# v in 512-byte runs with its key halves swapped on chip, and expert matrices loaded in halves through attention

## The chip, the cores and the metric

The kernel runs on one core of a Trainium2 chip. The metric is the device time of one execution in microseconds (us). All tensors are 32-bit floats. The compute engines are TensorE (PE in the profile; its weight loads are PEld), VectorE (DVE), ScalarE (ACT) and GpSimd (POOL). SyncE (SP) issues every transfer. Each engine works through its own list in order and waits, where it must, on semaphores of the others and of the transfers.

## The reference

Three stages follow each other: attention inside chunks of 64 positions, a soft mixture of eight experts over all 4608 tokens, and a two-layer softplus block.

```python
# q, k, v: (8 batches, 8 heads, 576 positions, 64)
scores = scale * q_c @ k_c.T            # per chunk of 64 positions, 9 chunks
attn = softmax(scores); out = attn @ v_c
x = out as (4608, 512)
logits = x @ phi                        # 512 x 32 slots, 4 per expert
d = softmax of logits over the tokens; slot_input = d.T @ x
h = relu(slot_input[e] @ w1[e]); slot_out[e] = h @ w2[e]     # 8 experts, 512x1024 and 1024x512
y = softmax of logits over the slots @ slot_out
return softplus(y @ w_in) @ w_out       # 512x2048 and 2048x512
```

The slot inputs are sums over all tokens, so no expert product can begin before the last attention output is known. The expert matrices themselves, 16 blocks of w1 and 16 of w2 of 1 MiB each, can be loaded at any time for which there is room.

## The kernel before

**Units and pairs.** Attention is done in 36 units of two heads by 512 positions; nine groups G of four units make up the tokens. Group 0 (`MIXED`) holds the ninth chunk of all eight batches, the other eight groups hold the first 512 positions of one batch each. Two units share one load of v: a pair, `pr = u // 2`. Pairs 2 to 17 are plain, pairs 0 and 1 are the mixed ones.

**Steps of a unit.** A transposes q and k on TensorE (L404), B copies the result to the tile T (ACT, L413), M copies one 64-partition half of T to the other (POOL, L421), S forms the scores (PE, L435), m0 and m1 subtract the maximum and write P (DVE, L446 and L452), x takes the exponential (ACT, L460), C and Ce transpose P (L468, L473), D multiplies by v (PE, L487) into the PSUM tile X, n0 and n1 divide by the row sum (DVE, L501 and L510), E and Ee transpose the output for the product with phi (L522, L529). The row sum comes with D: a column of ones stands behind the 64 columns of each v row (`VW` is 65), written once at the start. The F steps close a group.

**v.** `load_v` (L272) brings a plain pair by four transfers of 128 KiB, one per 128 positions, with one position per partition: each run in memory is one head's row, 256 bytes. There are three v buffers (`BUF`). The mixed pairs fill two of them with one joint load.

**The expert matrices.** Blocks of w1 and w2 go to slots named w0 to w7, g0 to g3, i0 to i3 and d0 to d4 (tables W1 and W2). The w, g and i slots are free through attention; a d slot is opened only when a pool of attention closes: d0 after the last A, d1 and d2 after the last S, d3 and d4 after the last D. The first five w2 blocks go to i0 to i3 and w7. Later w2 blocks, and the blocks of w_in and w_out, take over slots which an expert product has read (table AFTER). H (L932) multiplies by w1 and SO (L974) by w2; H starts with the slot inputs, after the end of attention, and SO after all of H.

**The order of the work** is made when the program is built: `issue` keeps a clock per engine, a cost per step (COST), a latency, and a rank, and always takes the step that can begin first. What it writes is the fixed list of every engine. A block of weights is a step `lw` with rank 100 and more, so SyncE gets it in gaps that q, k and v leave. A slot in SyncE's list then also waits for its turn: transfers use eight semaphores in turn, and a transfer that would reuse one waits for the transfer before it on that semaphore.

## Time and profile before

| what | value |
|---|---|
| median of 3 runs | 677.46 us (676.0 to 678.55) |
| profiled execution | 678.23 us, span 676.5 us |
| TensorE busy | 636.2 us, 94% of the span |
| VectorE, ScalarE, GpSimd busy | 432.2, 315.9, 237.2 us |
| transfers | 107.93 MB, 80543 packets, 42464 of them under 512 bytes |

The profiled execution lies 1.73 us above its span and 0.77 us above the median. A busy TensorE in this profile means that a matrix product is under way by a model of its pipeline, not that it runs at its peak. The attention stage lasts to about 176 us, H from 178 to 192 us, SO from 195 to 227 us, and the softplus block takes the rest.

### The profile page before, as it was taken

Reading aid. Unit: us, or ns where it says so; the run is one execution under the profiler, and the core shown is the slowest. Engines: PE = TensorE matmul, PEld = TensorE weight load, DVE = VectorE, ACT = ScalarE, POOL = GpSimd, SP = SyncE. Lnnn points to the kernel's source line nnn. Section 1 sums busy time; section 2 is a strip of 40 time slices with the busy share of each in tenths; the row PEclk is TensorE's granted clock in tenths of the full one; section 3 lists DMA queues with packets and bytes.
Section 4 is the critical chain, followed back from the end, with each engine's and each line's share of the span. In section 5 each row is a group of like instructions: output and inputs, shape, how many; then the busy total and the mean of one; then the engine's idle time right before and its main releaser. Section 6 shows DMA issues by size and latency. Waiting matters only on the chain.

```text
span 676.5 us, 14096 instructions
## 1 busy us (share of the span) xinstructions
PE 636.2 (94%) x5849; PEld 511.0 (76%) x5849; DVE 432.2 (64%) x634; ACT 315.9 (47%) x475; POOL 237.2 (35%) x205
## 2 busy tenths in 40 slices
PE   5899979887997899999999999999999999999997
PEld 4788768765453677888788788888888888888885
DVE  1678868775257699878877877754555554545551
ACT  2576546553133587734554755544333333333330
POOL 4233223220124436612222233444433344433341
PEclk7999989998999999999999999999999999999999
DMA  9799969999999904112313510222414223231412
GB/s 169 194 256 267 253 176 272 237 299 405 416 407 413 406 24 126 61 63 93 125 63 114 198 62 32 77 80 78 110 62 125 63 85 103 78 110 63 116 40 62
DMA packets 80543, 107.93 MB, mean 160 GB/s; under 512 B 42464, under 2 KB 60896, under 8 KB 78560
## 3 DMA queue, kind: packets, MB, share of 16 engines
q1 hardware_dynamic: 80480, 107.04, 49.5%
q8 instruction: 46, 0.75, 0.5%
q14 instruction: 17, 0.14, 0.1%
HBM read 88.15 MB, written 18.87 MB: 158 GB/s over the span
## 4 chain that ended last, share of the span: by engine, by line
PE 80%; DVE 8%; DMA 5%; issue 3%; ACT 2%; SPq 1%; POOL 1%; DVEq 0%; POOLq 0%; ACTq 0%
PE trm L1147 18%; PE trm L1145 18%; PE trm L1143 18%; PE ph L1085 5%; PE tr L404 4%; PE X L487 3%; PE tr L468 2%; PE S L435 2%; PE hps L932 2%; PE tr L522 2%; DMA i<-in_moe_w_dram 2%; PE tr L598 2%; DMA w5b<-in_moe_w_dram 2%; PE tr L540 1%; DVE nm L446 1%
## 5 line engine op out<-in xcount | busy, mean ns | idle before, releaser
L1124 POOL TENSOR_TENSOR g<-hTm,g 128x1024 fp32r<-128x1024 f32 (+1 forms) x37 | 86.8, 2348 | 105.1 <-ACT g L1120 101.5
L1110 ACT ACTIVATE hTm<-hTm 128x1024 f32<-128x1024 f32 (+2 forms) x51 | 51.5, 1012 | 79.9 <-DVE hTm L1104 79.7
L421 POOL COPY T<-T 64x512 f32<-64x512 f32 x72 | 43.9, 610 | 106.2 <-ACT T L413 105.3
L1104 DVE TENSOR_SCALAR hTm<-ph 128x1024 uint32<-128x1024 uint32 (+2 forms) x51 | 59.0, 1159 | 34.6 <-PE ph L1085 34.5
L1114 DVE SCALAR_TENSOR_TENSOR hTm<-ph,hTm 128x1024 f32<-128x1024 f32 (+1 forms) x37 | 44.1, 1194 | 23.5 <-ACT hTm L1110 23.5
L1120 ACT CAST g<-hTm 128x1024 fp32r<-128x1024 f32 (+1 forms) x37 | 37.9, 1026 | 41.1 <-DVE hTm L1114 41.1
L1159 DVE TENSOR_TENSOR i<-trm,i 128x512 f32<-128x512 f32 x52 | 35.7, 687 | 32.0 <-PE trm L1147 31.8
L413 ACT COPY T<-tr 128x512 f32<-128x512 f32 x72 | 41.0, 589 | 27.1 <-PE tr L404 26.8
L1085 PEld LDWEIGHTS ph<-cT,Tc 128*128 128x128 f32 x288 | 43.7, 190 | 10.1 <-issue 2.8
L1085 PE MATMUL ph<-cT,Tc 128*128 128x256 f32 x288 | 47.0, 286 | 0.9 <-DVE ph L1114 0.7
L1104 DVE TENSOR_SCALAR siT<-ph 128x1024 uint32<-128x1024 uint32 (+1 forms) x25 | 29.5, 1181 | 26.0 <-PE ph L1085 25.9
L1124 POOL TENSOR_TENSOR g<-siT,g 128x1024 fp32r<-128x1024 f32 x12 | 28.9, 2405 | 42.8 <-ACT g L1120 42.8
L1110 ACT ACTIVATE siT<-siT 128x1024 f32<-128x1024 f32 (+1 forms) x25 | 25.7, 1026 | 36.7 <-DVE siT L1104 36.7
L1124 DVE TENSOR_TENSOR g<-ph,g 128x1024 fp32r<-128x1024 f32 (+2 forms) x27 | 29.7, 1104 | 11.9 <-ACT g L1120 11.8
L404 PE MATMUL tr<-ident,q 128*128 128x128 f32 x144 | 29.8, 290 | 6.3 <-DMA q<-in_q_dram 5.2
L446 DVE TENSOR_REDUCE nm<-S 128x8 f32<-128x512 f32 x36 | 24.7, 686 | 16.4 <-PE S L435 16.3
L1120 ACT CAST g<-ph 128x1024 fp32r<-128x1024 f32 (+2 forms) x27 | 24.9, 921 | 19.5 <-DVE ph L1114 16.8
L435 PE MATMUL S<-T 64*64 64x64 f32 x1152 | 25.1, 224 | 7.9 <-DVE P L452 2.6
L435 PEld LDWEIGHTS S<-T 64*64 64x64 f32 x1152 | 21.0, 137 | 14.0 <-issue 9.9
L404 PE MATMUL tr<-ident,k 128*128 128x128 f32 x144 | 29.0, 284 | 0.2 <-DMA k<-in_k_dram 0.2
L460 ACT ACTIVATE P<-P 128x512 f32<-128x512 f32 x36 | 22.9, 638 | 11.4 <-DVE P L452 11.4
L452 DVE TENSOR_TENSOR P<-S,nm 128x512 f32<-128x512 f32 x36 | 24.4, 679 | 2.1 <-PE S L435 1.3
(439 smaller groups left out, 1741.7 us busy)
## 6 DMA issues: line engine op xcount, KB each, us to landing
part<-i SPq DMA_DIRECT2D x18, 512.0 KB, 2.6
i<-part SPq DMA_DIRECT2D x18, 512.0 KB, 3.9
q<-in_q_dram SPq DMA_DIRECT2D x32, 256.0 KB, 4.5
k<-in_k_dram SPq DMA_DIRECT2D x32, 256.0 KB, 4.8
vbm<-in_v_dram SPq DMA_DIRECT2D x40, 128.0 KB, 4.5
g<-in_moe_w_dram SPq DMA_DIRECT2D x5, 1024.0 KB, 8.2
d<-in_moe_w_dram SPq DMA_DIRECT2D x5, 1024.0 KB, 13.1
i<-in_moe_w_dram SPq DMA_DIRECT2D x5, 1024.0 KB, 13.7
```

The source lines that it names most:

```text
L404: nc.tensor.transpose(c, t[:, h, 2 * rr:2 * rr + 2, :].rearrange("p r d -> p (r d)"), ident)
L421: nc.gpsimd.tensor_copy(out=t[a:a + 64, :, 1], in_=t[b:b + 64, :, 2 * h])
L435: nc.tensor.matmul(out=sp[64 * o:64 * o + 64, b, 64 * i:64 * i + 64], lhsT=cs[:, 0], rhs=cs[:, 1], start=True, stop=True)
L1085: nc.tensor.matmul(out=ph(n, a, b)[:, j - a, :], lhsT=K["Tc"][:, f * 128:(f + 1) * 128], rhs=K["cT"][:, t * TT:(t + 1) * TT], start=True, ...
L1104: nc.vector.tensor_scalar(out=scratch(n, a, b).bitcast(U32), in0=ph(n, a, b).bitcast(U32), scalar1=0x80000000, scalar2=None, op0=ALU.bitwi ...
L1110: nc.scalar.activation(out=y, in_=y, func=AF.Softplus)
L1114: nc.vector.scalar_tensor_tensor(out=soft(n, a, b), in0=ph(n, a, b), scalar=0.0, in1=y, op0=ALU.max, op1=ALU.add)
L1120: nc.scalar.copy(out=V["gs", n][:, 0, a:b], in_=soft(n, a, b))
L1124: tt(e)(out=s[:, 1, a:b], in0=soft(n, a, b), in1=s[:, 0, a:b].bitcast(F32), op=ALU.subtract)
L1143: nc.tensor.matmul(out=po, lhsT=s[:, 0, j, ts_], rhs=wr[:, hs], start=(n in begin and j == 0), stop=False)
L1145: nc.tensor.matmul(out=po, lhsT=s[:, 0, j, ts_], rhs=wr[:, ls], start=False, stop=False)
L1147: nc.tensor.matmul(out=po, lhsT=s[:, 1, j, ts_], rhs=wr[:, hs], start=False, stop=(j == 3 and n in finish))
```

## The change

**v.** `load_v` now issues two transfers of 256 KiB. Two neighbouring positions of a head go to one partition, so a run is 512 bytes. A partition's tile part holds, per head, 130 numbers: a one, 64 of the even position, 64 of the odd position, a one. The ones around the first and the second row serve as the column of the row sum on either side.

**The swap.** With two positions per partition, 32 partitions hold one chunk of 64 keys. The product D needs each chunk on 64 partitions, so six new steps N per plain pair exchange blocks of 32 partitions (`st_N`): for each half of the partitions, upper even rows to a spare tile (POOL), lower odd rows to the upper even place (POOL), the spare tile to the lower odd place (ACT). The spare tile comes from the five `xT` buffers. D waits for the third and the sixth N. After the fifth, the first use of a buffer writes the ones. `lv` is given a lag of 2.5 in the planner.

**Scores and X.** S writes its chunks in another order for plain units, so m1 reads and writes without a permutation. D writes X with another column layout, and n0 and n1 read that layout.

**Halves.** Each block of w1 outside the d slots, and each of the first five w2 blocks, is two steps of 512 KiB in place of one of 1 MiB.

**Stores.** The output rows of all plain tiles go out in pieces of 64 rows.

```diff
     def load_v(t, pr):
         G, h0 = pr // 2, 4 * (pr % 2)
-        for m in range(4):
+        for b in range(2):
             nc.sync.dma_start(
-                out=t[:, m, :, 0:D],
-                in_=v[batch_of(G), h0:h0 + 4, 128 * m:128 * m + 128, :].rearrange(
-                    "h p d -> p h d"))
+                out=t[:, b, :, 1:2 * D + 1],
+                in_=v[batch_of(G), h0:h0 + 4, 256 * b:256 * b + 256, :].rearrange(
+                    "h (p r) d -> p h (r d)", r=2))
...
+    def st_N(pr, n):
+        def f(e, held):
+            t = V["vt", pr]
+            if n == 0:
+                V["vs", pr] = xp_.tile([128, 512], F32, tag=f"xT{held['xT', ('N', pr)]}", name="xT")
+            vtmp = V["vs", pr].rearrange("p (b h d) -> p b h d", b=2, h=4)
+            i, n_ = divmod(n, 3)
+            lo, up = slice(64 * i, 64 * i + 32), slice(64 * i + 32, 64 * i + 64)
+            dst, src = ((vtmp[lo], t[up, :, :, 1:1 + D]),
+                        (t[up, :, :, 1:1 + D], t[lo, :, :, 1 + D:VW + D]),
+                        (t[lo, :, :, 1 + D:VW + D], vtmp[lo]))[n_]
+            if e == "ACT":
+                nc.scalar.copy(out=dst, in_=src)
+            else:
+                nc.gpsimd.tensor_copy(out=dst, in_=src)
...
+        if G != MIXED and u % 2 == 0:
+            by["lv", pr].lag = 2.5
+            for n in range(6):
+                add("N", (pr, n), st_N(pr, n), [("lv", pr)] + [("N", (pr, n - 1))] * (n > 0),
...
-        add("D", u, st_D(u), [("Ce", u), ("lv", pr)],
+        add("D", u, st_D(u), [("Ce", u), ("lv", pr), ("N", (pr, 2)), ("N", (pr, 5))],
...
+    def halved(nm, n, sl, r):
+        add("lw", (nm, n, 0), at(load, nm, n, sl, 0), rank=r, cost={"SP": 1.35})
+        add("lw", (nm, n), at(load, nm, n, sl, 1), [("lw", (nm, n, 0))], rank=r, cost={"SP": 1.35})
+
     for n, sl in enumerate(W1):
         if sl[0] != "d":
-            add("lw", ("w1", n), at(load, "w1", n, sl), rank=100 + n)
+            halved("w1", n, sl, 100 + n)
     for n in range(5):
-        add("lw", ("w2", n), at(load, "w2", n, W2[n]), rank=130 + n)
+        halved("w2", n, W2[n], 130 + n)
...
-        if t % 2 == 0 and G != MIXED:
-            nc.sync.dma_start(out=out[rows[0]:rows[0] + 128, :], in_=o)
-            return
```

**Where the lists change.** SyncE's list around the last load of v, before: the tile `vb_116` of L272 is v, `w2a` and the others of L299 and L304 are w1 blocks.

```order
L265 DMA q<-in_q_dram 128x2x256
L265 DMA k<-in_k_dram 128x2x256
L304 DMA g_2789<-in_moe_w_dram 128x2048
L265 DMA q<-in_q_dram 128x2x256
L265 DMA k<-in_k_dram 128x2x256
L272 DMA vb_116<-in_v_dram 128x4x64 x4
L299 DMA w2a<-in_moe_w_dram 128x1024
L299 DMA w2b<-in_moe_w_dram 128x1024
L299 DMA w3a<-in_moe_w_dram 128x1024
L299 DMA w3b<-in_moe_w_dram 128x1024
L299 DMA w4a<-in_moe_w_dram 128x1024
L299 DMA w4b<-in_moe_w_dram 128x1024
```

The same place now (v is L273; a row of L302 or of L304 is half a block, `i_` is the tile of the first w2 blocks):

```order
L302 DMA w5b<-in_moe_w_dram 128x1024
L302 DMA w6a<-in_moe_w_dram 128x1024
L266 DMA q<-in_q_dram 128x2x256
L266 DMA k<-in_k_dram 128x2x256
L273 DMA vb_116<-in_v_dram 128x4x128 x2
L302 DMA w6b<-in_moe_w_dram 128x1024
L304 DMA g_3024<-in_moe_w_dram 128x1024
L304 DMA i_3048<-in_moe_w_dram 128x1024
L304 DMA i_3083<-in_moe_w_dram 128x1024
L304 DMA g_3024<-in_moe_w_dram 128x1024
L309 DMA d_3146<-in_moe_w_dram 128x2048
L304 DMA i_3048<-in_moe_w_dram 128x1024
```

Before, the last load of v has three g blocks, w0 and w1 ahead of it, 5 MiB of weights; now 19 halves, 9.5 MiB. Behind it a d block is no longer ahead of every i half. From the last two d blocks on (those that wait for the last D) to the last w2 block the list now holds 19 MiB.

GpSimd's list from the end of the start-up to the end of attention, before: 72 copies of T (M, L421) in one row.

```order
L754 MEMSET sel 128x64
L757 COPY sel<-ident 32x32 x4
L758 MEMSET one 1x1
L421 COPY T<-T 64x16x32 x72
L778 MEMSET siT 128x1152
L779 MEMSET hTm 128x2304
```

The same place now, its first twelve rows: between the copies of T (L447) stand copies of v (L414), from v to the spare tile `xT` and from v to v.

```order
L801 MEMSET one 1x1
L447 COPY T<-T 64x16x32 x12
L414 COPY xT<-vb_116 32x512
L414 COPY vb_116<-vb_116 32x8x64
L447 COPY T<-T 64x16x32 x2
L414 COPY xT<-vb_116 32x512
L447 COPY T<-T 64x16x32
L414 COPY vb_116<-vb_116 32x8x64
L416 MEMSET vb_116 128x8x2
L447 COPY T<-T 64x16x32 x2
L414 COPY xT<-vbm 32x512
L447 COPY T<-T 64x16x32
```

Each plain pair adds four such copies to this list and two to ScalarE's, where they stand between the copies B, x and Ce. From the second use of slot w0 on (w2 block 5) SyncE's list is the same in both programs, but for the smaller stores. On the other engines the second stage is planned anew from the other end of the first, and a few of its steps change places; on TensorE the transposes of the slot weights c (L851) move some places later, between the SO groups and the first `ph` products.

## Rows read from the trace of the kernel before

**Rows 1.** Busy time by stage; share, clock and DMA at the end of a row.

```profile
core 0: us, PE busy (x) PEld busy (x) DVE busy (x) ACT busy (x) POOL busy (x), PEclk, DMA share, GB/s
13.00:34.00 21.00, 17.89 (x364) 15.06 (x365) 11.98 (x24) 10.21 (x19) 6.09 (x10) 0.86 0.76 201
34.00:153.00 119.00, 106.67 (x2564) 88.40 (x2562) 89.89 (x202) 69.97 (x151) 35.98 (x59) 0.99 0.91 253
192.50:226.40 33.90, 28.22 (x308) 17.04 (x310) 22.07 (x32) 14.06 (x22) 11.33 (x8) 1.00 1.03 410
238.00:255.00 17.00, 16.61 (x76) 13.38 (x77) 16.81 (x27) 14.13 (x25) 6.82 (x5) 1.00 0.02 6
255.00:676.00 421.00, 416.55 (x1957) 344.22 (x1955) 264.59 (x285) 187.42 (x217) 160.00 (x82) 1.00 0.28 88
```

**Rows 2.** What TensorE waited for in 13 to 176 us: total, times, longest.

```profile
PE X L487 <- issue: 5.9, 3, 2.1
```

**Rows 3.** The chain of waits between the stages: start, duration, what.

```profile
178.11 13.91 PE hps L932 x128
...
211.16 12.66 DMA i<-in_moe_w_dram
...
223.86 1.06 PE sops L974 x8
...
226.41 1.10 PE sops L974 x16
```

**Rows 4.** SyncE in order of time: start, duration, operation, count.

```profile
139.45 5.50 SPq L272 DMA_DIRECT2D vb<-in_v_dram  x4
...
145.00 0.94 SPq L299 DMA_DIRECT2D w2a<-in_moe_w_dram  x1
...
168.02 0.80 SPq L304 DMA_DIRECT2D d<-in_moe_w_dram  x2
...
179.13 0.33 SPq L299 DMA_DIRECT2D w0a<-in_moe_w_dram  x1
```

**Rows 5.** DMA totals in 168 to 226.4 us: packets by size, share of the engines.

```profile
DMA packets 5241, 24.07 MB, mean 412 GB/s; under 512 B 556, under 2 KB 556, under 8 KB 4059
q1 hardware_dynamic: 5235, 23.98, 101.5%
```

**Rows 6.** DMA totals in 56 to 58.2 us, nearly all of it v.

```profile
DMA packets 1445, 0.37 MB, mean 168 GB/s; under 512 B 1434, under 2 KB 1445, under 8 KB 1445
q1 hardware_dynamic: 1445, 0.37, 73.2%
```

**Rows 7.** DMA totals in 17 to 20 us, nearly all of it q and k.

```profile
DMA packets 801, 0.77 MB, mean 256 GB/s; under 512 B 65, under 2 KB 800, under 8 KB 800
q1 hardware_dynamic: 800, 0.75, 85.1%
```

**Rows 8.** Costliest groups: the two copies of T; busy, mean ns, idle before.

```profile
L421 POOL COPY T<-T 64x512 f32<-64x512 f32 x72 | 43.9, 610 | 106.2 <-ACT T L413 105.3
L413 ACT COPY T<-tr 128x512 f32<-128x512 f32 x72 | 41.0, 589 | 27.1 <-PE tr L404 26.8
```

**Rows 9.** TensorE in order of time: products of P and v of four units.

```profile
31.07 0.70 PE L487 MATMUL X<-vbm,P 64*64 64x65 f32 x32 [0.23 <-DVE P L473]
...
44.57 0.68 PE L487 MATMUL X<-vbm,P 64*64 64x65 f32 x32
...
164.00 1.15 PE L487 MATMUL X<-vb,P 64*64 64x65 f32 x32
...
167.22 0.70 PE L487 MATMUL X<-vb,P 64*64 64x65 f32 x32
```

**Rows 10.** What the loads of q and k waited for in 13 to 176 us.

```profile
SPq L265 <- PE tr L404: 25.8, 19, 3.6
```

**Rows 11.** The tile of v: time from issue to landing.

```profile
DMA to landing us min/median/max: 2.3/4.6/8.9
```

**Rows 12.** GpSimd in order of time: the last piece of the first w_in block.

```profile
216.47 1.29 POOL L873 TENSOR_TENSOR g<-g,cvt 128x512 uint32<-128x512 uint32 x1 [2.04 <-DVE cvt L342]
```

More of the change, by code (lines that the diff above doesn't have):

```diff
@@ L73, in __init__ @@
         self.urgent = False
+        self.lag = 0.0
 def issue(steps, buffers, clock=None, held=None):
@@ L133, in issue @@
             port = clock[e]
-        s.end = clock[e] + LATENCY[e]
+        s.end = clock[e] + LATENCY[e] + s.lag
         for b, k in s.take:
@@ L243 @@
     vb2 = ap.tile([128, 2, 16 * VW], F32, name="vbm")
-    vb = [vb2[:, i].rearrange("p (m h e) -> p m h e", m=4, e=VW) for i in range(2)]
-    vb += [ap.tile([128, 4, 4, VW], F32, name=f"vb{i}") for i in range(2, NV)]
+    vb = [vb2[:, i].rearrange("p (b h e) -> p b h e", b=2, e=2 * VW) for i in range(2)]
+    vb += [ap.tile([128, 2, 4, 2 * VW], F32, name=f"vb{i}") for i in range(2, NV)]
     vm = vb2.rearrange("p i (m h e) -> p (i m) h e", m=2, e=VW)
@@ L284, in load_vm, with load @@
                     "x p d -> p x d"))
-    def load(nm, n, sl):
+    def load(nm, n, sl, part=None):
         e, i = divmod(n, 2)
@@ L295, in load @@
             src = w_out_u[256 * n:256 * n + 256, :].rearrange("(k p) f -> p k f", p=128)
-        parts = halves(sl)
+        parts = V["parts", nm, n] if part == 1 else halves(sl)
+        V["parts", nm, n] = parts
         if sl[0] == "w":
-            for t, x in zip(parts, (src[:, 0], src[:, 1])):
-                nc.sync.dma_start(out=t.bitcast(U32) if nm == "wo" else t, in_=x)
+            for i_, (t, x) in enumerate(zip(parts, (src[:, 0], src[:, 1]))):
+                if part in (None, i_):
+                    nc.sync.dma_start(out=t.bitcast(U32) if nm == "wo" else t, in_=x)
+        elif part is not None:
+            nc.sync.dma_start(out=parts[part], in_=src[:, part])
         else:
@@ L388, in f @@
                 return
-            V["v", pr] = vb[held["v", pr]]
-            load_v(V["v", pr], pr)
+            t = V["vt", pr] = vb[held["v", pr]]
+            V["v", pr] = lambda i, b, c, h: t[64 * i:64 * i + 64, b, h, VW * c:VW * c + VW]
+            load_v(t, pr)
+        return f
+    def st_N(pr, n):
[13 more added lines that the diff above has]
+                nc.gpsimd.tensor_copy(out=dst, in_=src)
+            if n == 4 and pr < 2 * MIXED + 2 + NV:
+                nc.gpsimd.memset(t[:, :, :, 0:2 * VW:2 * VW - 1], 1.0)
         return f
@@ L479, in f @@
             pt, vt = V.pop(("P", u)), V["v", u // 2]
[L480 to L496 removed]
+            for h in range(2):
+                for b in range(2):
+                    a = 64 * (h ^ b)
+                    for i, c in ((0, 0), (1, 1), (0, 1), (1, 0)):
+                        o = i ^ b
+                        x = 256 * c + 128 * h + (1 if c or u // HP == MIXED else 0)
+                        nc.tensor.matmul(
+                            out=xp[64 * o:64 * o + 64, b, x:x + VW],
+                            lhsT=pt[64 * i:64 * i + 64, 2 * b + c, a:a + 64],
+                            rhs=vt(i, b, c, 2 * (u % 2) + h),
+                            start=True, stop=True)
+        return f
     def st_n0(u):
         def f(e, held):
+            x = V["X", u][:, :, 0:1]
+            d, x0 = (256, D + 1) if u // HP == MIXED else (256 + D + 1, 0)
             z = V["z", u] = st_p.tile([128, 4, 2, 1], F32, tag="z", name="z")
[L501 removed]
+            nc.vector.tensor_scalar_add(
+                out=z.rearrange("p (b c) h o -> p b c (h o)", b=2),
+                in0=bass.AP(tensor=x.tensor, offset=x.offset + x0,
+                            ap=[*x.ap[0:2], [d, 2], [128, 2]]), scalar1=EPS)
             nc.vector.reciprocal(out=z, in_=z)
@@ L747 @@
     make_identity(nc, ident)
-    for t in vb:
-        nc.gpsimd.memset(t[:, :, :, D:VW], 1.0)
+    nc.gpsimd.memset(vm[:, :, :, D:VW], 1.0)
     for a in range(4):
@@ L1163, in st_oc @@
         G, m = t // 2, 2 * (t % 2) + i
-        if G == MIXED:
-            rows = [(m + 4 * j) * S + GT for j in range(2)]
-        else:
-            rows = [batch_of(G) * S + 128 * m + 64 * j for j in range(2)]
-        if t % 2 == 0 and G != MIXED:
-            nc.sync.dma_start(out=out[rows[0]:rows[0] + 128, :], in_=o)
-            return
-        for j, r in enumerate(rows):
+        for j in range(2):
+            r = (m + 4 * j) * S + GT if G == MIXED else batch_of(G) * S + 64 * (
+                4 * (t % 2) + 2 * j + i)
             p0 = 64 * (j ^ t % 2)
```

32 lines of the change are left out of this document (13 added, 19 removed), and 4 rows, old and new, of the table COST.

## The prediction

> **What bounds the kernel now.** I read the table by stage first, then the chain of waits across the two stage borders, then SyncE's own list in time, and last the DMA totals of a few short stretches. The reader is to see three regimes.
>
> From 255 us to the end TensorE is busy 416.55 of 421 us [rows 1]. Nothing in that stretch is changed but some stores, so it can only start earlier or later as a whole.
>
> Through attention TensorE is busy 106.67 of 119 us between 34 and 153 us, against 89.89 for VectorE, 69.97 for ScalarE and 35.98 for GpSimd; the DMA engines have a share of 0.91 [rows 1]. The largest item of TensorE's waits is 5.9 us in three gaps that are put down to "issue", that is, to no other engine [rows 2]. The loads of q and k, on the other side, waited 25.8 us for TensorE to free a buffer [rows 10]. So TensorE paces attention and transfers run ahead of it.
>
> Between attention and the softplus block it is the transfers. The chain goes through H from 178.11 to 192.0 us, then stands on weight transfers (12.66 us on an i block alone), and the last SO products run at 223.86 and 226.41 us [rows 3]. In 192.5 to 226.4 us the DMA share is 1.03 at 410 GB/s while VectorE has 22.07 and GpSimd 11.33 busy us in 33.9 [rows 1]. What counts there is how many bytes still stand in front of the last w2 block when the last attention product frees the last two d slots. From 168.0 us, when SyncE issues those two [rows 4], to 226.4 us 24.07 MB were moved at 412 GB/s, without a pause [rows 5].
>
> **The change part by part.** *Bytes behind the last D.* In SyncE's new list 19 MiB stand from those two d blocks to the last w2 block: 2 in d, 3 in i2, i3 and w7, 2 in w0 and w1, 2 of w_in, 5 in w2 to w6, 2 in g3 and i0, 1 of w_out, 2 in i1 and i2. That is 19.92 MB, and at 412 GB/s [rows 5] 48.4 us. Now the queue can run dry before, since the six and a half MiB between the last load of v and those d blocks take 6.82 MB / 412 GB/s = 16.5 us from about 145 us [rows 4], so to 162 us, less than 168. The list then restarts from an empty queue; the price is at least part of an issue-to-landing time, of which the shortest shown is 2.3 us [rows 11]; I take 2.0. So the last w2 block lands 50.4 us after 168.0, at 218.4 us, where before the last products began at 226.4 [rows 3]: **8.0 us less**. The ends: 10.0 us less without a restart, 1.1 less with one as long as the longest landing of v, 8.9 us [rows 11].
>
> That needs H to free slots early enough. The first reused slot, w0, was refilled at 179.13 us [rows 4], just behind the first H products at 178.11 [rows 3]. The five MiB of d, i2, i3 and w7 take 12.7 us from 170.0 and end at 182.7, so this wait is covered by 3.6 us, and H frees a block in 13.91 / 16 = 0.87 us where a transfer takes 2.55. No term.
>
> *Room for the halves in attention.* By the last load of v 9.5 MiB have been issued in place of 5, 4.72 MB more, 11.5 us of all DMA engines. A packet of v costs 0.732 x 2.2 us x 16 / 1445 = 17.8 ns [rows 6], a q or k packet of 1024 bytes (0.851 x 3 us x 16 - 65 x 17.8 ns) / 735 = 54 ns [rows 7]. A run of 512 bytes is not in this trace; it lies between these two, and beyond neither unless runs are cut. By bytes I take 17.8 + 36.2 / 3 = 30 ns. The 32768 runs of the plain pairs now take 36.5 us of all engines; 16384 runs of 30 ns take 30.7, 5.8 less (bounds 18.3 less and 18.8 more). Room left by the shares is 0.24 x 21 + 0.09 x 119 = 15.7 us [rows 1]. So 21.5 us stand against 11.5: **no term**; with the upper bound the halves do not quite fit, and up to 14.6 us would be missing. Half blocks also hold up a following q load for 1.3 us of transfer in place of 2.5, which I count as nothing.
>
> *The swap.* Per plain pair four GpSimd copies at 610 ns and two ScalarE copies at 589 ns, by the nearest rows, the two copies of T [rows 8]: 3.6 us one behind the other. In all 64 x 0.61 = 39 us on GpSimd and 32 x 0.589 = 19 us on ScalarE, which has 69.97 of 119 busy [rows 1]; GpSimd's idle time before its copies of T alone is 106.2 us [rows 8]. D of the pair waits for all six, and so do the copies of T queued behind a copy that waits for its v; S of a later unit waits for those. Neither wait is in this trace. The lower bound is nothing. The upper bound is every chain exposed, 16 x 3.6 = 58 us.
>
> Where is the cover thin? At the first buffers that are freed by the mixed pairs. The last mixed D starts at 31.07 us and the next D on such a buffer at 44.57 us [rows 9], 12.8 us after the first has ended. Into that must now go two issues, 0.80 us as those of the two d blocks [rows 4], a landing of 4.6 us [rows 11], and 3.6 us of copies, 9.0 us. It is covered with 3.8 us to spare, but a copy of T may stand behind two of the new ones: I take 2 x 0.61 = **1.2 us more**, once. Later there is plenty: the last four transfers of v are issued from 139.45 us [rows 4] for a D at 164.00 us [rows 9]. I take the value near nothing because TensorE, with 90% busy and gaps of its own, is later than everything that feeds it, so a late feeder is absorbed as long as it is late by less than its lead.
>
> *Other edits.* The 1152 score products, the transposes and the D products stay as many as they were. m0, m1, n0 and n1 read the same number of elements. The ones are three small memsets. Sixteen more stores in the last stage are beside a DMA share of 0.28 [rows 1]. None has a term; I allow 1 us either way.
>
> *Behind SO.* All loads after the last w2 block follow each other in the same list, so they come earlier by the same 8 us. The conversions of the first w_in block ended at 217.76 us [rows 12], 8.7 us before the last SO, and that block too comes earlier; VectorE is idle 11.8 us of 33.9 there [rows 1], enough to lose 7. From 238 to 255 us VectorE is busy 16.81 of 17 [rows 1], so what is not done by then would be paid: 0, bound 3 us.
>
> Sum against the profiled execution: 678.23 - 8.0 + 1.2 = 671.4 us. That execution lies 0.77 us above the median, so the forecast for a median is 670.7; **671 us**.
>
> **The rivals.** *B, GpSimd's queue becomes the wait, and the kernel is slower.* The new copies are first in line for a v that has not landed, the copies of T behind them wait, S waits for T, and TensorE stands. For it speaks that GpSimd is in order and that TensorE has no slack to catch up (rows of 90% and over). Against it speak the lead of v, 24.6 us at the last pair, and a GpSimd that is idle more than half the time. The weights' gain of 8 us is spent when each of 16 pairs costs 0.5 us. At one exposed copy of 0.61 us and one ScalarE copy per pair it is 16 x 1.2 = 19 us: 677.5 - 8 + 19 = 688 us; at two thirds of that, 682.
>
> *C, the gain stays off the path.* Either the halves only take DMA time that q, k and v needed and attention ends 5 to 8 us later, or they stand in SyncE's list behind loads that wait for a buffer [rows 10] and land no earlier than before, so that the change does not do what it says. The time is then 677.5 - 8 + 6 = 675.5, up to 678. For it speaks the share of 0.91; against it that q and k wait for TensorE and not the reverse.
>
> *D, transfers pace attention more than it seems.* Then what v saves shortens it, 5.8 us, beside the 8 us: 677.5 - 13.8 = 664 us. Against it is that the loads waited for buffers. By the Trainium skill (DMA: Bandwidth & Descriptors, Specifications) a transfer of at least 512 bytes runs at line rate. By that rule v's 8.39 MB would go at the weights' 412 GB/s and take 20.4 us, 16 less than now; under rival D the time would be 653 us, in my sum it would only widen the room. The trace of before has no such run to weigh it by.
>
> **How the numbers follow.** My forecast has 0.56, its own range 667 to 675; B 0.14, C 0.17, D 0.13. A measurement of this kernel tells about 0.5% from no change, 3.4 us, so faster means below 674.1 us: nearly all of the forecast (0.53 of 0.56) and D, 0.66. The same takes the rest of the forecast and most of C, 0.19. Slower is B and a little of C, 0.15. The range reaches from D's 664 to just below B's middle, 680; beyond lie about 0.08 below and 0.11 above.
>
> **What would show it.** Right: in the chain of waits the last SO products begin at about 219.5 us, attention's last D at 168 to 170, TensorE's busy share between 34 and 153 us stays near 0.9, the DMA share falls below 1 for some us before the last d blocks, and the stretch from the last SO to the end keeps its 450 us. Packets under 512 bytes fall by about 32,800, and those of 512 take some 30 ns. Wrong: D or S with waits for GpSimd or ScalarE of half a us and more per pair; a last D after 173 us; a DMA share of 1 up to a last SO after 224 us; or a stretch behind SO that is longer by what was gained.

## The result and the profile after

The changed kernel took 684.12 us in the median of 16 executions (680.04 to 689.13), the kernel before 677.02 us (16, 674.83 to 681.98). The ratio is 1.0099 with an interval of 1.0078 to 1.0121: **1% slower**, where 671 us and "faster" had been forecast. The profiled execution took 681.23 us with a span of 679.4, so it is one of the quicker ones: it shows 3.0 of the 7.1 us. What the slower ones lose beyond that is in no trace.

The table by stage after (start and end of the stretch, its length, busy us and instructions per engine, granted clock, DMA share, GB/s) answers [rows 1]:

```profile
34.00:153.00 119.00, 106.01 (x2502) 87.80 (x2500) 91.03 (x208) 81.52 (x168) 69.29 (x116) 1.00 0.90 278
192.50:226.40 33.90, 31.23 (x355) 18.38 (x348) 20.76 (x38) 16.67 (x27) 13.66 (x8) 0.95 1.02 410
238.00:255.00 17.00, 15.30 (x71) 12.00 (x72) 15.00 (x24) 13.81 (x26) 6.92 (x5) 1.00 0.11 36
255.00:676.00 421.00, 419.18 (x1968) 346.29 (x1967) 268.11 (x287) 188.87 (x218) 160.28 (x82) 1.00 0.29 86
```

The regimes are those of before. GpSimd's busy time in attention has nearly doubled (35.98 before), TensorE's has not moved, 25 GB/s more were carried; but behind SO, at 238 to 255 us, TensorE does 1.31 us less than before.

The chain of waits at the stage borders (start, duration, what) answers [rows 3]:

```profile
182.79 4.52 PE hps L975 x32
...
210.94 13.37 DMA i<-in_moe_w_dram
...
224.35 1.06 PE sops L1017 x8
225.41 1.49 PE hps L958 x6
226.90 1.10 PE sops L1017 x16
```

SyncE in order of time answers [rows 4]:

```profile
171.67 0.81 SPq L309 DMA_DIRECT2D d<-in_moe_w_dram  x2
...
184.68 0.33 SPq L302 DMA_DIRECT2D w0a<-in_moe_w_dram  x1
...
193.30 0.34 SPq L302 DMA_DIRECT2D w2a<-in_moe_w_dram  x1
```

The 3.0 us can be added up from stage borders of the two traces. The last D begins at 170.7 us where it was 167.2 [rows 9]: **+3.5**. From there to the first H product are 12.1 us where there were 10.9: **+1.2**; the row for 174.2 to 184.7 us below, in which TensorE was busy for 9.29 of 10.50 us, has a granted clock of 0.84, so a part of it is at the lower of the two levels, 1.2 GHz. From H to the end of SO are 45.2 us where there were 49.4 (227.51 - 178.11 [rows 3]): **-4.2**. From the end of SO to the end of TensorE are 446.8 us where there were 444.3: **+2.5**. The saving exists, and three other places take more than it.

The table by stage after, in finer stretches behind the last D, shows where transfers paused:

```profile
168.00:171.70 3.70, 3.70 (x74) 3.29 (x67) 1.71 (x5) 0.59 (x1) 0.00 (x0) 0.60 0.74 300
171.70:174.20 2.50, 2.50 (x40) 2.18 (x39) 0.93 (x3) 0.58 (x1) 0.00 (x0) 1.00 0.65 116
174.20:184.70 10.50, 9.29 (x71) 6.12 (x73) 3.52 (x12) 2.01 (x7) 3.06 (x2) 0.84 1.00 405
184.70:193.30 8.60, 8.60 (x84) 2.40 (x80) 2.46 (x7) 0.86 (x2) 0.00 (x0) 1.00 0.93 306
193.30:226.80 33.50, 30.83 (x348) 18.24 (x340) 20.00 (x35) 16.34 (x27) 13.99 (x9) 0.95 1.03 411
```

The queue ran dry before the d blocks, as forecast, and its restart cost 2.5 x (1 - 116 / 412) = 1.8 us. It slumped again at 184.7 to 193.3 us, just from the first reissue of a slot that H frees (w0a at 184.68): 8.6 x (1 - 306 / 412) = 2.2 us.

The copies, by line and shape (count, busy us, mean ns, idle time before them and its releasers), answer [rows 8]:

```profile
L414 POOL COPY xT<-vbm 32x512 f32<-32x512 f32 x20 | 12.3, 616 | 2.2 <-DVE fm L588 1.0
...
L414 POOL COPY xT<-vb 32x512 f32<-32x512 f32 x12 | 7.4, 613 | 2.2 <-DMA vb<-in_v_dram 1.6
```

```profile
L412 ACT COPY vbm<-xT 32x512 f32<-32x512 f32 x20 | 12.4, 621 | 1.2 <-POOL vbm L414 0.9
```

A copy costs 0.61 to 0.62 us, as taken. And TensorE waited for them hardly at all; its waits from 13 to 176 us (total, times, longest), which answer [rows 2]:

```profile
PE S L462 <- issue: 4.8, 4, 2.6
PE tr L430 <- DMA q<-in_q_dram: 3.8, 1, 3.8
PE X L519 <- issue: 3.4, 2, 1.8
...
PE S L462 <- POOL T L447: 0.6, 1, 0.6
...
PE S L462 <- POOL xT L414: 0.3, 1, 0.3
```

### The profile page after: what moved, and what is told of

The parts are those of the page before. It is cut to its first block, busy times and chain, and to the rows that moved or that the text cites. A ratio compares the mean times of both kernels' runs of the same rounds, so it can differ in the third digit from the quotient of the medians.

```text
span 679.4 us, 14230 instructions
## 1 busy us (share of the span) xinstructions
PE 640.0 (94%) x5849; PEld 513.5 (76%) x5849; DVE 431.3 (63%) x637; ACT 333.6 (49%) x504; POOL 278.6 (41%) x270
## 4 chain that ended last, share of the span: by engine, by line
PE 78%; DVE 7%; DMA 6%; issue 3%; ACT 3%; SPq 1%; POOL 1%; ACTq 0%; DVEq 0%; POOLq 0%
PE trm L1186 18%; PE trm L1188 18%; PE trm L1190 18%; PE ph L1128 5%; PE tr L430 4%; PE X L519 3%; PE S L462 3%; PE tr L555 2%; PE tr L501 2%; DMA i<-in_moe_w_dram 2%; DMA g<-in_moe_w_in_dram 2%; DMA w5b<-in_moe_w_dram 2%; PE tr L631 1%; PE tr L573 1%; DMA q<-in_q_dram 1%
## 5 line engine op out<-in xcount | busy, mean ns | idle before, releaser
L447 POOL COPY T<-T 64x512 f32<-64x512 f32 x72 | 43.8, 608 | 63.5 <-ACT T L439 61.6
L1128 PEld LDWEIGHTS ph<-cT,Tc 128*128 128x128 f32 x288 | 43.7, 190 | 10.9 <-issue 1.9
L1167 POOL TENSOR_TENSOR g<-siT,g 128x1024 fp32r<-128x1024 f32 x12 | 28.9, 2404 | 42.5 <-ACT g L1163 42.5
L462 PE MATMUL S<-T 64*64 64x64 f32 x1152 | 26.6, 225 | 10.3 <-issue 4.8
L501 PE MATMUL tr<-ident,P 128*128 128x128 f32 x144 | 23.4, 286 | 3.5 <-ACT P L493 2.1
```

Of the source, the lines that this page charges most:

```text
L447: nc.gpsimd.tensor_copy(out=t[a:a + 64, :, 1], in_=t[b:b + 64, :, 2 * h])
L462: nc.tensor.matmul(out=sp[64 * o:64 * o + 64, b, 64 * k:64 * k + 64], lhsT=cs[:, 0], rhs=cs[:, 1], start=True, stop=True)
L1128: nc.tensor.matmul(out=ph(n, a, b)[:, j - a, :], lhsT=K["Tc"][:, f * 128:(f + 1) * 128], rhs=K["cT"][:, t * TT:(t + 1) * TT], start=True, ...
L1167: tt(e)(out=s[:, 1, a:b], in0=soft(n, a, b), in1=s[:, 0, a:b].bitcast(F32), op=ALU.subtract)
```

## The experiments

All ratios are to the kernel before, run beside the kernel in question; times of stages are from one profiled execution of each. "34 to 60" is TensorE's busy time in that stretch of 26 us, the first in which only plain units run.

| kernel | v's cost | ratio (95%) | last D | first H | SO ends | 34 to 60 |
|---|---|---|---|---|---|---|
| before | 2.7 | 1 | 167.2 | 178.1 | 227.5 | 25.55 |
| changed | 2.1 | 1.0099 (1.0078 to 1.0121) | 170.7 | 182.8 | 228.0 | 21.73 |
| e1 no copies | 2.1 | 1.0132 (1.0092 to 1.0173) | 172.4 | 184.1 | 228.3 | 20.73 |
| e2 halves only | 2.7 | 1.0030 (1.0002 to 1.0058) | 164.1 | 177.0 | 227.0 | 25.55 |
| e3 v only | 2.1 | 1.0206 (1.0158 to 1.0253) | 179.0 | 190.3 | 234.0 | 21.80 |
| e4 second list of before | 2.1 | 1.0091 (1.0055 to 1.0126) | 176.0 | 187.2 | 231.5 | 20.90 |
| e5 copies planned free | 2.1 | 1.0159 (1.0113 to 1.0204) | 177.4 | 189.1 | 235.2 | 22.70 |
| e6 before, late v planned | 2.7 | 0.9990 (0.9960 to 1.0021) | 163.3 | 175.6 | 225.1 | 25.08 |
| e7 e4 and e5 joined | 2.1 | 1.0200 (1.0158 to 1.0242) | 180.7 | 191.4 | 239.4 | 23.09 |
| e8 weights held back | 2.1 | 1.0125 (1.0079 to 1.0172) | 171.2 | 183.5 | 235.4 | 21.18 |
| f1 old order in D | 2.1 | 1.0079 (1.0050 to 1.0108) | 170.1 | 181.3 | 225.6 | 21.62 |
| f2 before, new lists | 2.1 | 1.0137 (1.0109 to 1.0166) | 175.9 | 187.3 | 233.4 | 21.08 |
| f3 before, weights ahead | 2.7 | 1.0016 (0.9992 to 1.0040) | 164.1 | 176.0 | 223.3 | 25.55 |
| g1 changed, old cost | 2.7 | 1.0049 (1.0020 to 1.0077) | 168.0 | 180.9 | 230.2 | 25.08 |
| g2 before, new cost | 2.1 | 1.0080 (1.0045 to 1.0116) | 172.5 | 184.0 | 229.6 | 21.42 |
| g3 e6 and weights ahead | 2.7 | 1.0072 (1.0045 to 1.0098) | 171.4 | 182.0 | 231.9 | 24.83 |
| g4 g1 and weights ahead | 2.7 | 1.0021 (0.9990 to 1.0051) | 167.7 | 178.5 | 227.8 | 24.74 |
| h1 before, tail emptied | 2.7 | 1.0074 (1.0044 to 1.0104) | 181.7 | 193.5 | 237.0 | 25.11 |
| h2 g4, tail emptied | 2.7 | 1.0191 (1.0149 to 1.0233) | 179.7 | 192.1 | 234.6 | 23.91 |
| i1 g1 without copies | 2.7 | 1.0059 (1.0031 to 1.0086) | 164.6 | 177.4 | 228.0 | 25.08 |

The profile of h1 is the longest of its 12 executions (690.21 us, median 682.03), so its stage times are not typical and nothing below rests on them.

One trace does not fix the last D. e4 has the lists of the changed kernel on every engine up to that point, and its last D begins 5.3 us later; e7 stands so to e5 with 3.2 us. f3 and e2, which share the kernel before's compute lists in attention but not its transfers, have it 3.1 us earlier. The column "34 to 60" moves by 0.8, 0.4 and nothing in these pairs. So 3 to 5 us between two last D are no effect by themselves. Taken together the last D do separate: with v at 2.1 all ten begin at 170.1 us or later, with 2.7 all but g3, h1 and h2 at 168.0 or earlier.

### Are the copies, or the halves, the cost?

e1: the six copies of each pair are left out of the changed kernel, so the swap is missing; lists, weights and layouts stay.

```diff
-            if e == "ACT":
-                nc.scalar.copy(out=dst, in_=src)
-            else:
-                nc.gpsimd.tensor_copy(out=dst, in_=src)
```

> The changed kernel with the same lists on every engine, but the six copies of each swap leave nothing in the lists of GpSimd and ScalarE (the swap of key halves is left out, so the 16 plain groups compute with v rows in the wrong places). Theory 1 (the copies hold up the copies of T and so the scores): attention falls back, the last D from 170.7 to about 167 us, and the time to 677 us or below, ratio to before 0.995 to 1.000, since the weights' gain of about 4 us stays. Theory 2 (the new order of the lists and TensorE's half-clock stretches make attention longer, the copies cost nothing): the time stays at 683 to 684 us, ratio 1.009 to 1.010, last D at 170 to 171 us.

1.0132, and the last D at 172.4 us: no gain. The copies are not the cost.

e2, the halves alone in the kernel before:

```diff
-            add("lw", ("w1", n), at(load, "w1", n, sl), rank=100 + n)
+            halved("w1", n, sl, 100 + n)
...
-        add("lw", ("w2", n), at(load, "w2", n, W2[n]), rank=130 + n)
+        halved("w2", n, W2[n], 130 + n)
```

> The kernel before with the expert blocks of the first use in halves and nothing else changed: v in 256-byte runs, no swap. Theory A (the bytes that stand in front of the last w2 block are what the middle stage waits for, as forecast): more MB are moved by the last load of v, the last SO begins 3 to 6 us before 226.4 us, and the time is 672 to 675 us, ratio 0.993 to 0.997. Theory B (with v in short runs there is no room in attention, q and k come late or the halves land no earlier): 677 us, ratio 0.999 to 1.005.

1.0030. In this list only 4 MiB stand ahead of the last v, not 9.5, so halves alone don't bring weights forward.

e3 is e2's edit the other way round, on the changed kernel: whole blocks.

> The changed kernel with whole blocks of 1 MiB in the first use: v in 512-byte runs with the swap, no halves. If the halves gave about 4 us back in the changed kernel (theory A), this is slower than it, 687 to 689 us, ratio 1.014 to 1.018. If the halves give nothing (theory B) it is the same as the changed kernel, 684 us, ratio 1.010; and if they cost time through attention, it is below, 679 to 681 us, ratio 1.003 to 1.006.

1.0206: without halves the changed kernel is worse still, with a last D at 179.0 us.

### Is it the planned place of the copies, the second list, or the weights?

e4 plans the second stage of the changed kernel from the clock at which the first stage of the kernel before ended:

```diff
-    clock = issue(steps, dict(BUF, tr=4, S=2, X=1, dT=1))
+    issue(steps, dict(BUF, tr=4, S=2, X=1, dT=1))
+    clock = {"SP": 169.8, "PE": 150.06, "POOL": 133.34, "ACT": 149.03, "DVE": 151.24, None: 141.54}
```

> The changed kernel, but the second stage is planned from the end times of the first stage in the kernel before, so that behind attention every engine has the list of before, word for word. In the profile the stretch from the last SO to the end was 452.5 us where it had been 450.1. Theory of the new second list: those 2.4 us go, 681.5 us, ratio 1.006. Theory that the stretch is longer for its clock or its later data: 684 us, ratio 1.010.

1.0091 is not to be told from 1.0099. In the trace the stretch behind SO went from 446.8 back to 445.1 us. The three other kernels with the changed kernel's second list (e1, f1, f2) have 446.8 to 446.9 us there too, and the kernel before and eleven with other second lists 444.3 to 444.4, so by the traces most of that 2.5 us is the new second list (e3, h1 and h2 also lie above 446, without it); the times don't resolve it.

e5 plans the copies as if they cost nothing:

```diff
-            by["lv", pr].lag = 2.5
+            by["lv", pr].lag = 0.0
...
-                    {"ACT": 0.6} if n % 3 == 2 else {"POOL": 0.67})
+                    {"ACT": 0.01} if n % 3 == 2 else {"POOL": 0.01})
```

> The changed kernel with all its work, but the lists are planned as if the six copies of a swap cost 0.01 each and v needed no lag, so D and the other steps of attention stand nearly as in the kernel before. Theory O (attention is longer because D stands later in the lists and other steps are moved ahead of it, not because the copies take time): the last D comes back to 165 to 168 us, the last SO begins 43 to 44 us after the first H, at 221 to 223 us, and the time is 672 to 676 us, ratio 0.993 to 0.999. Theory P (the copies need their planned place; without it copies of T stand behind a v that has not landed): attention is longer still, the time is 686 us and more, ratio 1.013 and up.

1.0159: no gain. e7 joins it with e4's edit:

> The kernel of the run e5_copies_planned_free with, behind attention, the lists of the kernel before word for word. If the new second list costs the 1.7 us that stand between the last SO and the end in the profiles (446.8 us with it, 445.1 without), this is 0.002 to 0.003 below e5_copies_planned_free in ratio; else the same.

1.0200, clear of the changed kernel: planning the copies where they can't be done makes the lists worse, and there was no loss behind SO left to win back (444.4 us in e7 and in e5).

e6 gives the kernel before a list in which v is planned 9 us late:

```diff
+            if G != MIXED:
+                by["lv", pr].lag = 9.0
```

> The kernel before with the same work and the same transfers, but its lists are planned as if v came 9.0 later in the planner's clock, so that D of each plain pair stands later, about as in the changed kernel. Theory O: TensorE gets more gaps over half a us, the last D comes 3 to 6 us later than 167.2 us, and the time rises to 679 to 683 us, ratio 1.004 to 1.010 (the weights run dry for some of it, so not all of the delay shows). Theory Q (the order is innocent; the weights in attention or the clock do it): the same as before, 0.998 to 1.003.

0.9990, with a last D at 163.3 us. A list that is planned for a late v is not bad for that.

e8 holds all blocks beyond the first five behind the last load of v in the changed kernel:

```diff
-        add("lw", (nm, n, 0), at(load, nm, n, sl, 0), rank=r, cost={"SP": 1.35})
+        late = [("lv", NU // 2 - 1)] if (nm, n) not in [("w1", i) for i in range(5)] else []
+        add("lw", (nm, n, 0), at(load, nm, n, sl, 0), rank=r, cost={"SP": 1.35}, after=late)
```

> The changed kernel, but all expert blocks behind the first five MiB are planned after the last load of v, as in the kernel before; attention's other steps keep nearly the same places. Theory Q (the transfers of weights in attention hold up q, k and v): attention is 3 to 5 us shorter, last D at 166 to 168 us. Theory O: attention stays as in the changed kernel, last D at 170 to 175 us, and without the weights ahead the last SO comes 4 to 8 us later than there; the time is 688 to 692 us, ratio 1.017 to 1.022.

Attention stays as long (last D 171.2), so there is no sign that the added weights lengthen it; by the scatter named above, one trace can't exclude 3 us. SO ends 7.4 us later, but 1.0125 and 1.0099 overlap.

### Is it the lists or the layouts?

f1 puts D's sixteen products per half back into the order of before:

```diff
-            for h in range(2):
-                for b in range(2):
-                    a = 64 * (h ^ b)
-                    for i, c in ((0, 0), (1, 1), (0, 1), (1, 0)):
+            for c in range(2):
+                for h, b, i in ((h, b, i) for h in range(2) for b in range(2) for i in range(2)):
+                        a = 64 * (h ^ b)
```

> The changed kernel, with the sixteen matrix products of a plain D in the order of the kernel before (the two positions outermost, then head, half of the row, chunk), in which no two products in a row use the same quarter of the array; operands, places and lists are those of the changed kernel. Theory R (D's new order costs some 0.05 us in each of 36 D, and what follows from it): the last D begins at 167 to 169 us instead of 170.7, and the time is 2 to 4 us shorter, 680 to 682. Theory L (the lists that the planner wrote make attention longer): the last D stays at 170 to 172.5 us, and the time within 1 us of the changed kernel's 684.

1.0079, last D at 170.1: neither is resolved from the changed kernel.

f2 is the kernel before with the plan of the changed one. N emits nothing:

```diff
-    "lq": {"SP": 1.7}, "lv": {"SP": 2.7}, "lwi": {"SP": 1.35},
+    "lq": {"SP": 1.7}, "lv": {"SP": 2.1}, "lwi": {"SP": 1.35},
...
+            by["lv", pr].lag = 2.5
+            for n in range(6):
+                add("N", (pr, n), lambda e, held: None,
...
-            add("lw", ("w1", n), at(load, "w1", n, sl), rank=100 + n)
+            halved("w1", n, sl, 100 + n)
```

> The kernel before (256-byte runs of v, its places of S, m1, D and X, no swap), planned as the changed kernel is: v at 2.1 us and a lag of 2.5 us, six steps N per plain pair that emit nothing, blocks in halves. Its lists on TensorE, ScalarE and SyncE are then those of the changed kernel without its copies. Theory L (the lists make attention longer): the last D begins at 170 to 173 us as in the changed kernel (170.7) and in the one without copies (172.4), and the ratio to the kernel before is 1.008 to 1.015. Theory R or any other of the new places and shapes: the last D begins at 166 to 168 us as before, with 9.5 MiB of weights ahead of the last v, the last SO ends at 222 to 224, and the ratio is 0.993 to 0.998.

1.0137, last D at 175.9: with the old runs, layouts and no copy, the new lists alone make the kernel slower. The first line of this diff is a part of the change that its description ahead of the prediction leaves out: in COST a load of v went from 2.7 to 2.1 us of SyncE.

### One number of the planner

g1 is the changed kernel with that number put back, g2 the kernel before with that number alone changed:

```diff
-    "lq": {"SP": 1.7}, "lv": {"SP": 2.1}, "lwi": {"SP": 1.35},
+    "lq": {"SP": 1.7}, "lv": {"SP": 2.7}, "lwi": {"SP": 1.35},
```

> The changed kernel whole (512-byte runs, swap, new places, halves), with one number of the planner put back: a v load costs 2.7 us in COST as before, not 2.1. Its list on TensorE then runs with that of the kernel before for longer, and 5.5 MiB of weights are ahead of the last v instead of 9.5. Theory C (the cost of v in the planner, by letting weights and q, k move in its list, makes the long attention): the last D begins at 164 to 168.5 us instead of 170.7, and the ratio to the kernel before is 0.998 to 1.004. Theory N (planning the copies N makes the list bad): the last D at 170 to 173, and with fewer weights ahead the ratio 1.010 to 1.016.

> The kernel before with that one number changed: a v load costs 2.1 us in COST, not 2.7. Nothing else is touched, no halves, no swap, 256-byte runs. 9 MiB of weights are then ahead of the last v. Theory C: the last D begins at 170 to 176 us, and the ratio is 1.006 to 1.016, the whole of what the change does. Theory N: the last D stays at 166 to 168.5 us, the last SO ends 3 to 5 us earlier than 227.5, and the ratio is 0.993 to 0.998.

g2 is slower by 0.80%: one number, in a kernel that is else untouched, does nearly all that the change does. g1 takes back half of the 0.99%, and its interval ends just below the changed kernel's (1.0077 against 1.0078). In its trace the stretch behind SO is back at 444.4 us, so the second list, which is planned from the end of the first, may be 2.5 of the 3.4 us that come back. The place in attention can be seen. The row of 34 to 60 us by stage, kernel before, then g2, then g1:

```profile
34.00:60.00 26.00, 25.55 (x624) 21.26 (x626) 20.32 (x46) 17.93 (x39) 9.77 (x16) 1.00 0.97 245
```

```profile
34.00:60.00 26.00, 21.42 (x519) 17.75 (x512) 16.58 (x38) 12.87 (x26) 6.74 (x11) 0.93 0.82 213
```

```profile
34.00:60.00 26.00, 25.08 (x602) 21.14 (x599) 19.89 (x44) 21.42 (x46) 19.96 (x35) 1.00 0.88 267
```

TensorE starts 105 products fewer in those 26 us in g2, every engine does less, and the transfers too. The last column of the table above separates the kernels without overlap: 23.91 to 25.55 us with v at 2.7, 20.73 to 23.09 with 2.1, whatever else was edited. SyncE's list shows what moved (start, duration, operation). Before, then g2:

```profile
28.60 5.25 SPq L272 DMA_DIRECT2D vbm<-in_v_dram  x4
...
36.00 3.51 SPq L272 DMA_DIRECT2D vbm<-in_v_dram  x4
```

```profile
31.75 0.46 SPq L299 DMA_DIRECT2D w0a<-in_moe_w_dram  x1
32.26 0.42 SPq L299 DMA_DIRECT2D w0b<-in_moe_w_dram  x1
32.73 4.43 SPq L272 DMA_DIRECT2D vbm<-in_v_dram  x4
...
40.31 2.12 SPq L272 DMA_DIRECT2D vbm<-in_v_dram  x4
```

With v cheaper the planner puts a further pair of q and k and a weight block ahead of the second plain pair's v, which goes out at 32.73 in place of 28.60 us, and it writes TensorE's list for that: D later, transposes of later units earlier. In the changed kernel that load stands at 34.06 us. How that list loses time differs from trace to trace. TensorE's three largest waits in 24 to 60 us (total, times, longest), in g2 and then in the changed kernel:

```profile
PE tr L468 <- issue: 2.5, 1, 2.5
PE S L435 <- issue: 1.6, 1, 1.6
PE S L435 <- DVE P L452: 0.8, 3, 0.3
```

```profile
PE tr L501 <- ACT P L493: 1.4, 1, 1.4
PE tr L501 <- issue: 1.3, 1, 1.3
PE S L462 <- DVE P L480: 1.2, 1, 1.2
```

The kernel before and g1 have no wait for "issue" in this stretch. In g2 nearly all of the lost 4.1 us are two such waits, and 3.5 us at the lower clock come on top (last section); in the changed kernel waits for ScalarE and VectorE are the larger part. A later D by itself is not it: in the trace of e6, 18 of the 72 steps A stand ahead of the fifth D, in g2 17 and in the kernel before 15, and e6 keeps its 25.08 us. So that the number costs time is shown by g2's ratio; which places of the new list cost it is not.

i1 is g1 without the copies (the swap is left out):

> The changed kernel planned with v at 2.7 us (g1), and the steps N emit no copies: the swap is left out, all lists but GpSimd's and ScalarE's copies are those of g1. g1 stands at 1.0049 of the kernel before. If the copies themselves cost what is left there: ratio 0.997 to 1.002, last D 165 to 167 us. If what is left is in the lists, the places or the shape of v's loads: ratio 1.003 to 1.007, last D 167.5 to 169.

1.0059 against g1's 1.0049: in good lists too the copies cost nothing that can be measured, though the last D comes 3.4 us earlier in i1's trace. Its SO ends at 228.0 all the same. Its rows by stage suggest why:

```profile
60.00:153.00 93.00, 83.75 (x1964) 68.05 (x1963) 71.46 (x159) 52.31 (x113) 27.45 (x45) 1.00 0.81 250
...
168.00:228.00 60.00, 52.24 (x517) 28.29 (x517) 29.65 (x56) 18.50 (x33) 17.33 (x12) 0.97 1.02 410
```

The transfers idle for a fifth of attention and are then full for 60 us: in this trace they set the end of SO, and the shorter attention buys nothing.

### What are weights ahead worth?

f3 keeps all lists of the kernel before, and issues w2 to w6 as ten halves, one behind each v load of pairs 6 to 15:

```diff
             load_v(V["v", pr], pr)
+            if 6 <= pr <= 15:
+                n, part = divmod(pr - 6, 2)
+                load("w1", 10 + n, W1[10 + n], part)
```

> The kernel before with its lists unchanged on every compute engine; on SyncE alone the blocks w2 to w6 go out earlier, one half block of 512 KiB behind each of the v loads of pairs 6 to 15, in place of all ten halves behind the last v load. 10 MiB are then ahead of the last v, as in the changed kernel. Theory L: attention keeps its length (last D 167 to 168.5 us), the last SO ends 4 to 5 us earlier than 227.5, and the ratio is 0.993 to 0.996. If weights ahead cost attention what they save: last D 170 to 172, last SO at 226 to 228, ratio 0.998 to 1.003.

1.0016: 10 MiB ahead of the last v, and nothing gained over the executions, although in the profiled one, the quickest of 12, SO ended 4.2 us early. g3 is the same on e6, g4 the same on g1:

> A candidate: the kernel before, planned with v landing 9 us later (in the profiled run that list gave the last D at 163.3 us and a ratio of 0.999), and the ten halves of w2 to w6 issued one behind each v load of pairs 6 to 15. If weights ahead are worth what the profiles of the two kernels say (last SO 2 us nearer to H): the last SO ends at 221.5 to 224, ratio 0.992 to 0.997. If attention gives it back, as the median of the kernel before with these halves ahead let one suppose (1.0016): ratio 0.998 to 1.003.

> A second candidate: the changed kernel with v at 2.7 us in COST, its lists on the compute engines unchanged by it, and the ten halves of w2 to w6 issued one behind each v load of pairs 6 to 15, so that 10 MiB are ahead of the last v with 512-byte runs. Theory C with weights ahead at their worth: last D 165 to 169, last SO 46 to 48 us behind the first H product instead of 49.5, ratio 0.993 to 0.999. If attention gives it back: ratio 0.999 to 1.004.

g3 loses 0.7%; e6's short attention is gone (last D 171.4). g4 stands at 1.0021 and can't be told from g1 or from the kernel before. Its trace, then that of before, from the last load of v to the last D:

```profile
145.00:168.00 23.00, 20.82 (x505) 16.36 (x505) 17.97 (x41) 16.73 (x38) 9.79 (x16) 1.00 0.61 210
```

```profile
145.00:168.00 23.00, 17.32 (x369) 13.63 (x369) 13.32 (x32) 9.19 (x20) 3.05 (x5) 0.93 0.97 366
```

The five MiB that g4 loads early had their place here before, in time in which nothing more urgent could be sent, since the d blocks next in line wait for the last S and D. Loaded early, they leave the DMA engines idle here.

h1 and h2 therefore also move the first five w2 blocks ahead of the d blocks (on f3 and on g4):

```diff
+            if pr == 17:
+                for n in range(5):
+                    load("w2", n, W2[n])
```

> The kernel before, lists of all compute engines unchanged; on SyncE the ten halves of w2 to w6 go out one behind each v load of pairs 6 to 15 (as in f3), and the five first w2 blocks (i0 to i3 and w7) behind the last v load, ahead of the five d blocks instead of behind them. Theory U (only bytes behind the last D's slots count: f3 moved weights out of 145 to 168 us, where the transfers had nothing more urgent, and so gained nothing): now 5 MiB leave the stretch behind the last d block (24.07 MB there before), the first reissue of w0 still waits for H at 179 to 180 us, and the last SO ends at 219 to 223 us instead of 227.5; ratio 0.989 to 0.995. If H's slots or something else end the stretch: last SO at 225 to 228, ratio 0.997 to 1.003.

> The same on the changed kernel planned with v at 2.7 us (g4 with the five first w2 blocks behind the last load of v): 512-byte runs, swap and all else of the change. Theory U: last D 167 to 169, last SO 43 to 45 us behind the first H product (g4: 49.3, g1: 49.3), ratio 0.993 to 0.998, and the change then gains what the prediction had put to it. If not: as g4, ratio 1.000 to 1.005.

The stretch from H to the end of SO does fall in h2, to 42.5 us, where g4 has 49.3. But both are slower, 1.0074 and 1.0191. In h2 q and k of the last unit stand behind those five MiB, and TensorE's largest wait in 135 to 182 us is for them:

```profile
PE tr L436 <- DMA q<-in_q_dram: 9.7, 1, 9.7
```

And behind attention the transfers are short of work until H, which begins at 192.1 us, frees slots; h2 by stage:

```profile
188.00:198.00 10.00, 9.02 (x83) 4.00 (x79) 2.14 (x6) 0.18 (x1) 3.06 (x2) 1.00 0.36 116
```

So weights that are early shift the wait to H, which can't start before attention ends. No kernel of the study beats the kernel before by more than the measurement can tell.

## Why the prediction was wrong

**Bytes behind the last D (-8.0 us).** Right in kind, mis-sized. From the issue of the last two d blocks to the landing of the last i block are 52.6 us (171.67 to 224.31); I had 50.4. Before, that landing was at 211.16 + 12.66 = 223.82 us [rows 3], 55.8 us after the issue. The gain is 3.2 us. Of the missing 4.8, 2.6 are an error of mine: I set a landing in the new kernel against the start of the last SO products (226.4) in the old one, though some 2.6 us of products follow the landing in both. The other 2.2 are the slump at 184.7 to 193.3 us. The restart, taken as 2.0, cost 1.8.

**"That needs H to free slots early enough ... No term."** This step failed as well: the refill of w0 moved with H, from 179.13 to 184.68 us, and the queue slumped there by the 2.2 us just named.

**Swap (+1.2 us) and rival B.** The cost of a copy was right and the cover held: e1 and i1 find no gain without the copies. Rival B is not what happened, although its sign was: TensorE's waits for GpSimd add up to little over 1 us in attention.

**"Other edits ... None has a term; I allow 1 us either way."** This is the step that turned the sign. No cost of an edit of the tiles was found where one was tested (the copies, D's order), but I priced the work of the lists and not their order. The planner's cost of v rewrites the lists of all engines, the last D comes 3.5 us later and the second list takes 2.5 us more in the profile, and g2 shows that this number alone makes the kernel before 0.8% slower. That lists changed was on view ahead of the prediction; I read in them how many bytes stand where, and not when D and v come.

**"Behind SO: 0, bound 3 us."** +2.5 us, inside the bound and at its wrong end. The prediction looked there for data that come late; what the traces show is the new second list. In h2, where SO comes closest behind H, 7.9 us lie between the end of SO and the first product of the softplus block (234.6 to 242.5 us), where g4 and the kernel before have 4.4: TensorE waits 2.4 us there for VectorE. An SO that ends sooner behind H may thus not keep all that it gains; as h2's second list differs in places from theirs, this is not shown.

**Rivals C and D.** C comes nearest: the gain was spent elsewhere, though there is no sign that the halves took q's or k's time (e8). Its "not the reverse" overlooked one wait of TensorE for q, 5.2 us before 24 us in the kernel before. For D, and the rule of the Trainium skill that the prediction named beside it (DMA: Bandwidth & Descriptors, Specifications: line rate from 512 bytes on), one microsecond of the changed kernel, 100.7 to 101.7 us, holds almost nothing but v:

```profile
DMA packets 363, 0.19 MB, mean 186 GB/s; under 512 B 0, under 2 KB 363, under 8 KB 363
## 3 DMA queue, kind: packets, MB, share of 16 engines
q1 hardware_dynamic: 363, 0.19, 66.5%
```

A run of 512 bytes took 0.665 x 16 us / 363 = 29 ns of an engine, my 30, and at a share of 1 that is 186 / 0.665 = 280 GB/s, where the weights go at 410. Here the rule does not hold, and a packet of v costs what the forecast took.

**What stays open.** With v's cost put back, 0.5% remain (g1, i1). The copies are not it; the planned steps N, the halves (e2 has 0.3%, barely told from nothing), the layouts and the stores were not taken apart there. Nor is it known where executions slower than the profiled ones lose their time, though one pair with equal lists gives a hint: from 13 us to the last D, TensorE in e4 is busy 2.9 us longer than in the changed kernel for the same products, at a mean clock of 0.95 against 0.98, and waits 3.1 us more for "issue".

## What to carry to other kernels

A number in a planner's cost table is an edit of every engine's list: change it alone and time that before the rest. An earlier transfer is worth only what it takes out of a stretch in which the transfers are the last to end; ask what the DMA engines will do in the time that it leaves, and which slot they then wait for. Compare a landing with a landing.

## What the runs showed that I had not expected

TensorE's waits put down to "issue" differ strongly with what is queued on the DMA engines. In 135 to 182 us D alone waited 3.8 us so in the kernel before, which has six MiB queued there, and 0.3 us in f3, which has the same compute lists and one MiB. They cut through groups; in g2 (start, duration, operation, idle time before):

```profile
37.73 0.49 PE L468 MATMUL tr<-ident,P 128*128 128x128 f32 x3
40.74 0.47 PE L468 MATMUL tr<-ident,P 128*128 128x128 f32 x1 [2.52 <-issue]
...
42.00 1.15 PE L487 MATMUL X<-vb,P 64*64 64x65 f32 x32
```

The fourth product of a group of four starts 2.5 us late, with nothing to wait for that the profile shows, and the same 32 products of D that take 0.70 us elsewhere take 1.15 behind it. The rows by stage of g2:

```profile
38.20:40.30 2.10, 0.02 (x1) 0.00 (x0) 0.15 (x1) 0.90 (x2) 0.55 (x1) 1.00 0.94 231
40.30:43.80 3.50, 3.06 (x53) 2.56 (x57) 1.21 (x4) 0.59 (x1) 0.61 (x1) 0.51 1.07 281
```

TensorE did next to nothing for 2.1 us, and then ran 3.5 us at a granted clock of 0.51, the lower level.

Counted along TensorE's list, these waits stand on a grid. The twenty traces have 113 of them over 0.6 us up to the last D, and 103 begin within five products of number 470 plus a whole multiple of 125.6, where chance would put nine in a hundred. The wait in g2 above is at number 470; seven of the other nine kernels with v at 2.1 have one of 1.3 to 2.2 us there, and none with 2.7 has. So the place in the list sets where such a wait can fall, and executions of one list differ in which of these places cost time (number 470 took 1.3 us in the changed kernel and 2.1 in e4). That instructions arrive in blocks, and that transfers of weights delay a block, would fit, but was not tested by itself.
